# A spectral block with a Mish MLP on one core: column matrices by POOL's converting DMA, another order at the start

## The chip, the cores and the metric

The kernel runs on one core of one Trainium2 chip. The core has five engines that run side by side and wait for each other through semaphores: TensorE (PE in the profile; PEld is its loading of weights), VectorE (DVE), ScalarE (ACT), GpSimd (POOL) and SyncE (SP, which here only issues DMAs). Sixteen DMA engines move data between the chip's memory (HBM) and the core's. Each engine works through its own queue of instructions in order; an instruction that waits holds up all that stand behind it on that engine.

The metric is the device time of one execution in microseconds (us); lower is better. Three runs of the kernel before took 402.98, 403.83 and 403.90, median 403.83.

## The reference

The input x is 2048 rows of 512 numbers. Six rows of 512 numbers, `sa, ca, ga, sb, cb, gb`, are computed from a conditioning vector c.

```python
mod = (silu(c) @ w_mod).reshape(c.shape[0], 6, 1, -1)
h = layernorm(x) * (1 + ca) + sa
x = x + ga * irfft2(rfft2(h) * (w_r + 1j * w_i))      # over rows and columns
h = layernorm(x) * (1 + cb) + sb
x = x + gb * (mish(h @ w1 + b1) @ w2)                 # 512 -> 1376 -> 512
```

All is float32. The change lies in the forward transform `rfft2` (and, with one line, in the first product of `h @ w1`).

## The kernel before

**Stages.** The span has four: the forward transform of the rows and the first part of that of the columns (tiles n = 0 to 15, up to about 56 us), the rest of the column transform with the multiplication by the filter (to about 110), the inverse transform (to about 160), and the MLP in eight blocks (to the end). Each stage is written out by hand in the order in which its instructions stand in the queues (`tc.manual_schedule()`); nothing reorders them, and the framework adds the semaphore waits.

**The first stage.** Row 16 p + n of x stands on partition p of tile n, so a tile is 128 rows of 512 numbers. For every tile:

- `load_all` has SP issue three DMAs: `xring` (the tile of x, transposed on the host, eight buffers), `x` (the tile itself) and `mraw` (the tile's column matrix, 128 x 256: real and imaginary part; 128 KB).
- `norm_sums` takes mean and variance on DVE (L112, L113). `norm_guess` (ACT, L117 and L118) makes a first value of one over the deviation, `norm_refine` (DVE, three short instructions at L125) improves it, for two tiles at a time.
- `p1_row` is the row transform on PE (L192, four fp32 products; the matrix `krs` already holds the factor 1 + ca). `p1_mean` (DVE, L207) takes the mean's part away, with the row `kb` that `row_sums` and ACT's copy L203 made once.
- `p1_cast` and `p1_low` scale the result and split it in a high part `gh` and a low part `gl`, both float32r, the format in which PE takes 32-bit numbers in fewer passes: even tiles with ACT (L220) and DVE (L227), odd tiles with ACT (L216, L217) and POOL (L218).
- `p1_split` splits the column matrix in the same way: ACT casts `mraw` to the high part (L184), POOL subtracts for the low part (L185) and turns the sign of the imaginary parts (L186). The ring `mring` has eight buffers.
- `p1_col` is the column product on PE, nine matmuls: (high matrix, `gh`), (low matrix, `gh`), (high matrix, `gl`), each as L234, L235 and L236. `p1_save` (ACT, L240) takes the result out of PSUM.

In the loop, iteration n holds `p1_save(n-1)`, `p1_row(n+2)`, `p1_mean` and `p1_cast` of tile n + 1, `p1_low(n)`, `p1_col(n)`, `p1_split(n+3)` and `norm_sums(n+3)`.

**Before the loop.** c and the scale's weights `wmc` are loaded by ACT and SP, c is passed through silu (the last step is L298 on DVE, which makes `sc`), PE runs eleven products of ones (`warm`, L273), then sixteen products that give the scale as columns (`scale_sums`, L245, 128 equal columns of which one is used), and DVE makes `krs` from them (`scale_rows`, four at L250).

**The shift sums.** `mod_step` (DVE, L97 and L99) adds up the shift row sa from four pieces of `wms`: the pieces at iterations 12, 13, and the last two at 14. `shift_columns` after the loop needs the sum (PE, L104).

**DMA queues.** The framework has eight semaphores for the DMAs issued by SP and ACT, so a DMA waits until the one eight before it has landed. SP also issues, in the first stage, `wms` and the second stage's weights (`load_rest`: `kf`, `wz`, `wqa` and others). POOL issues no DMA in this kernel.

**The first product of the MLP.** `up(g)` multiplies by the high part of w1 (L729, 512 columns: high and low half of h) and by its low part (L731, the 256 columns of h's high half). `up(0)` and `up(1)` stand in the last tiles of the inverse transform, where `p3_row` (PE, L647) is followed by an addition to x on DVE (L650).

Of the kernel before, what the change touches and what calls it, by code (L numbers as in the profile page):

```python
# [7 lines left out]
F32 = mybir.dt.float32  # L8
F32R = mybir.dt.float32r
# [21 lines left out]
def tile_spectral_block(ctx: ExitStack, tc: tile.TileContext, x_d, w1_d, b1_d, w2_d,  # L31
# [24 lines left out]
    def plain(t):  # L56
        return t.bitcast(F32)
# [15 lines left out]
    eps = base.tile([P, 1], F32, name="eps")  # L73

    saz = base.tile([P, NQ], F32, name="saz")
    mraw = big.tile([P, N2, 256], F32, name="mraw", tag="da")
    mring = big.tile([P, 8, 2, 384], F32R, name="mring", tag="db")
    wmc = big.tile([P, 4, 512], F32, name="wmc", tag="cr")
    wms = big.tile([P, 4, 512], F32, name="wms", tag="ci")

# [29 lines left out]
    def norm_sums(n):  # L110
        t = small.tile([P, 6], F32, name="st")
        nc.vector.bn_stats(t, x[:, n, :])  # L112
        nc.vector.bn_aggr(mv[:, n, :], t)  # L113
# [31 lines left out]
        return h  # L145

    st = {}
    mkd = km_d.bitcast(F32R)

    def mt(n):  # L150
        return mring[:, n % 8]

    def load_m(n):
        nc.sync.dma_start(mraw[:, n, :], km_d[:, n, :])

    def load_x(n):
        nc.sync.dma_start(x[:, n:n + 1, :], xv[:, n:n + 1, :])

    def load_xt(n):
        t = xring[:, n % 8]  # L160
        nc.sync.dma_start(t, xt_d[n])
        st["xt", n] = t

    def load_all(n):
        load_xt(n)
        load_x(n)
        load_m(n)

    def load_rest():
        nc.sync.dma_start(ident, kp_d)  # L170
# [8 lines left out]
                nc.sync.dma_start(b1n[:, 0:NF - 1], b1_d[0:(NF - 1) * P].rearrange("(f p) -> p f", p=P))  # L179
                nc.sync.dma_start(b1n[0:F - (NF - 1) * P, NF - 1:NF], b1_d[(NF - 1) * P:F].unsqueeze(1))  # L180

    def p1_split(n):
        m = mt(n)
        nc.scalar.copy(m[:, 0, 0:256], mraw[:, n, :])  # L184
        nc.gpsimd.tensor_tensor(m[:, 1, 0:256], mraw[:, n, :], plain(m[:, 0, 0:256]), op=ALU.subtract)  # L185
        nc.gpsimd.tensor_scalar(m[:, :, 256:384], plain(m[:, :, 128:256]), -1.0, 0.0,  # L186
                                op0=ALU.mult, op1=ALU.add)

    def row_products(pg, data):
# [39 lines left out]
    def p1_col(n):  # L229
        m = mt(n)  # L230
        gh, gl = st.pop(("g", n))
        pa = bank("C")
        for i, (a, g) in enumerate(((0, gh), (1, gh), (0, gl))):
            nc.tensor.matmul(pa, m[:, a, 0:128], g, start=(i == 0), stop=False)  # L234
            nc.tensor.matmul(pa[:, 0:256], m[:, a, 256:384], g[:, 256:512], start=False, stop=False)  # L235
            nc.tensor.matmul(pa[:, 256:512], m[:, a, 128:256], g[:, 0:256], start=False, stop=(i == 2))  # L236
        st["pa", n] = pa

    def p1_save(n):
# [2 lines left out]
    def scale_sums(ks, ps):  # L242
        for k in ks:
            for j in range(4):
                nc.tensor.matmul(ps[j][:, 0:P], wmc[:, k, j * P:(j + 1) * P], sc[:, k:k + 1].to_broadcast([P, P]),  # L245
                                 start=(k == 0), stop=(k == 3))

    def scale_rows(ps):
        for j in range(4):
            nc.vector.scalar_tensor_tensor(krs[:, j, :], kr[:, j, :], ps[j][:, 0:1], kr[:, j, :],  # L250
                                           op0=ALU.mult, op1=ALU.add)
# [23 lines left out]
    with tc.manual_schedule():  # L275
        def load_scale(eng, k):
            eng.dma_start(wmc[:, k, :], wm_d[:, 1, k, :])

        nc.scalar.dma_start(sc, c_d.rearrange("b (p k) -> p (b k)", k=4))
        load_scale(nc.scalar, 1)  # L280
        load_scale(nc.scalar, 3)
        nc.scalar.preload_act_table_set("natural_log_exp_and_others")
        load_xt(0)
        load_scale(nc.sync, 0)
        load_scale(nc.sync, 2)
        nc.sync.dma_start(kr, kr_d)
        load_x(0)
        load_m(0)
        for n in range(1, 8):
            load_all(n)  # L290
        nc.vector.memset(ones, 1.0)
        nc.vector.memset(eps, EPS)
        nc.vector.memset(b1n[:, NF - 1:NF], 0.0)
        sg = small.tile([P, 4], F32, name="sg")
        nc.scalar.activation(sg, sc, AF.Exp, scale=-1.0)
        nc.vector.tensor_scalar(sg, sg, 1.0, None, op0=ALU.add)
        nc.vector.reciprocal(sg, sg)
        nc.vector.tensor_tensor(sc, sc, sg, op=ALU.mult)  # L298
        warm(11)
        cps = [bank(t) for t in "DDCC"]  # L300
        for k in range(4):
            scale_sums((k,), cps)
        norm_sums(0)
        norm_guess(0, 1)
        scale_rows(cps)
        norm_refine(0, 1, -1)
        p1_split(0)
        p1_row(0)
        load_all(8)
        row_sums()  # L310
        p1_row(1)
        load_all(9)
        norm_sums(1)
        norm_guess(1, 2)
        p1_mean(0)
        p1_cast(0)
        norm_refine(1, 2, -1)
        p1_split(1)
        p1_mean(1)
        p1_cast(1)  # L320
        p1_low(0)
        p1_split(2)
        norm_sums(2)
        for n in range(N2):
            if n >= 1:
                p1_save(n - 1)
            if n + 2 < N2:
                p1_row(n + 2)
                if n + 10 < N2:
                    load_all(n + 10)  # L330
                if n == 4:
                    nc.sync.dma_start(wms, wm_d[:, 0, :, :])
                if n == 6:
                    load_rest()
            if 1 <= n and n + 1 < N2:
                p1_mean(n + 1)
                if n % 2:
                    norm_refine(n + 1, n + 3, -1)
                p1_cast(n + 1)
            if n:  # L340
                p1_low(n)
            p1_col(n)
            if n + 3 < N2:
                p1_split(n + 3)
                norm_sums(n + 3)
                if n % 2 == 0:
                    norm_guess(n + 2, n + 4)
            for k in {12: (0,), 13: (1,), 14: (2, 3)}.get(n, ()):
                mod_step(macc, wms[:, k, :], k, nc.vector)
        p1_save(N2 - 1)  # L350
        shift_columns()

# [368 lines left out]
    def up(g):  # L721
        b, t = item(g)
        h = h2[b]
        ups[g] = []
        for e, f, rows in tiles(t):
            ps = bank("CD"[e] if g < 2 else "AD"[e])[:rows]
            fs = slice(f * P, f * P + rows)
            for k in range(4):
                nc.tensor.matmul(ps, w1h[:, k, fs], h[:, k], start=(k == 0), stop=False)  # L729
            for k in range(4):  # L730
                nc.tensor.matmul(ps[:, 0:256], w1l[:, k, fs], h[:, k, 0], start=False, stop=(k == 3))  # L731
            ups[g].append((e, f, ps))

    def front(g):
# [208 lines left out]
def _constants():  # L943
# [11 lines left out]
    kr = pair(unit(512, (4 * a[:, None, None] + d2[None, :, None]) * q), 2)  # L955
    kr[:, :, 1, 0] = alt[:, None]
    z = unit(2048, (16 * a[:, None, None] + k2[None, :, None]) * a)
    km = np.stack([z.real, z.imag], 2)
    z = np.conj(z).transpose(2, 1, 0)
    kc = np.stack([z.real, -z.imag], 1)  # L960
    z = 2 * np.conj(unit(512, (4 * a[None, None, :] + d2[None, :, None]) * q[:, None, None]))
# [57 lines left out]
    def bwd(n, fn):  # L1019
# [5 lines left out]
    out = dict(kr=kr.reshape(128, 4, 128), km=km.reshape(128, 16, 256), kc=kc,  # L1025
               ki=ki.reshape(128, 4, 128), kf=kf, kv=kv, kw=kw, kp=np.eye(128))
    return {k: np.ascontiguousarray(v, dtype=np.float32) for k, v in out.items()}

# [48 lines left out]
```

## Time and profile before

| | |
|---|---|
| median of three runs | 403.83 us (402.98 to 403.90) |
| profiled execution, its own time | 403.98 us |
| span of that execution | 402.0 us, granted TensorE clock 1.00 |
| busy: PE, DVE, ACT, POOL | 390.5, 305.0, 249.9, 99.2 us |
| DMA | 36.45 MB, mean 91 GB/s |
| DVE busy in 20 to 30, 30 to 40, 40 to 50 us | 9.64, 9.72, 9.79 of 10 us |
| PE busy in the same | 9.34, 9.34, 9.36 |
| POOL busy in the same | 8.27, 7.46, 7.40 |

The page of the profile shows one execution: the busy time of each engine, the span in 40 slices (a digit is the busy share in tenths), the DMA queues, the chain of waits that ended last, and the costliest groups of instructions. The timeline gives each instruction with its start and length in us; a bracket names the idle time of the engine before it and what ended it. Matmuls are pipelined and their ends are modelled, so the distance of two starts says more of PE than its busy time. A row of the windows view gives a stretch, its length, the busy time of PE, PEld, DVE, ACT and POOL with counts in parentheses, the granted clock, the busy share of the DMA engines and GB/s.

### The profile page before, as it was taken

The page shows a single profiled execution, that of the slowest core. Times are in us where ns is not written, and L with a number is a line of the kernel's source. Part 1 is how long each engine was busy: PE and PEld are TensorE (multiplying, and loading weights), DVE is VectorE, ACT ScalarE, POOL GpSimd, SP SyncE. Part 2 cuts the span into 40 slices and gives each one's busy share as a digit, 9 for nine tenths or more (in the row PEclk, how much of TensorE's full clock was granted, in tenths as well). Part 3 has the DMA queues.
Part 4 walks back from the last instruction along what each step waited for, and adds up shares of the span by engine and source line. Part 5 has one row for each costly group of instructions (what it writes and reads, how often), then busy time and mean ns, then how long its engine had stood idle before and what let it go on. Part 6 is the DMA issues. An engine that isn't in the chain of part 4 may idle for free.

```text
span 402.0 us, 7454 instructions
## 1 busy us (share of the span) xinstructions
PE 390.5 (97%) x2782; PEld 360.5 (90%) x2782; DVE 305.0 (76%) x653; ACT 249.9 (62%) x547; POOL 99.2 (25%) x132
## 2 busy tenths in 40 slices
PE   8999979999999999999999999999999999999996
PEld 8888868999899999899899899899899899999984
DVE  2899958786339999887974974974974974987994
ACT  2577753667746954896494494494484484494751
POOL 0587725666316762230000000000000010017000
PEclk9999999999999999999999999999999999999999
DMA  8999790454304331100010010010010020023011
GB/s 286 382 334 389 207 314 7 127 215 176 94 14 122 90 124 48 62 18 2 9 45 2 4 50 0 2 53 2 0 55 2 0 72 2 2 78 132 1 54 52
DMA packets 20580, 36.45 MB, mean 91 GB/s; under 512 B 3680, under 2 KB 6528, under 8 KB 20160
## 3 DMA queue, kind: packets, MB, share of 16 engines
q1 hardware_dynamic: 20112, 35.45, 25.9%
q8 instruction: 22, 0.36, 0.4%
q10 hardware_dynamic: 432, 0.53, 0.4%
q14 instruction: 14, 0.11, 0.1%
HBM read 31.78 MB, written 4.19 MB: 89 GB/s over the span
## 4 chain that ended last, share of the span: by engine, by line
PE 74%; DVE 19%; ACT 3%; issue 2%; POOL 1%; POOLq 0%; ACTq 0%
PE bank L782 23%; PE bank L729 19%; PE bank L731 10%; DVE st L112 4%; PE bank L456 3%; DVE ve L125 3%; PE bank L502 3%; PE bank L774 3%; DVE x L650 2%; PE bank L794 2%; PE bank L489 2%; PE bank L616 2%; PE bank L435 1%; DVE buf L227 1%; DVE buf L207 1%
## 5 line engine op out<-in xcount | busy, mean ns | idle before, releaser
L739 ACT ACTIVATE buf<-bank,b1n 128x256 f32<-128x256 f32 (+1 forms) x88 | 40.9, 472 | 66.9 <-PE bank L731 66.7
L740 DVE TENSOR_TENSOR buf<-buf,bank 128x256 f32<-128x256 f32 (+1 forms) x88 | 35.4, 417 | 38.9 <-ACT buf L739 38.9
L689 DVE TENSOR_TENSOR al<-buf,ah 128x512 fp32r<-128x512 f32 (+2 forms) x85 | 53.4, 651 | 1.8 <-ACT ah L688 1.8
L706 POOL TENSOR_TENSOR buf<-buf,modr 128x512 f32<-128x512 f32 (+1 forms) x3 | 3.9, 1292 | 183.5 <-DMA buf<-in_B_w_dram 183.5
L729 PE MATMUL bank<-h2e,w1h 128*128 128x512 f32 (+1 forms) x176 | 48.4, 397 | 0.0
L729 PE MATMUL bank<-h2o,w1h 128*128 128x512 f32 (+1 forms) x176 | 48.3, 396 | 0.0
L688 ACT CAST ah<-buf 128x512 fp32r<-128x512 f32 (+2 forms) x85 | 43.0, 549 | 0.7 <-DVE buf L756 0.6
L756 DVE TENSOR_TENSOR buf<-buf 128x128 f32<-128x128 f32 x148 | 39.3, 307 | 3.5 <-ACT buf L746 2.2
L746 ACT ACTIVATE buf<-buf 128x512 f32<-128x512 f32 (+1 forms) x48 | 28.7, 598 | 14.9 <-DVE buf L740 14.8
L782 PE MATMUL bank<-w2a,ah 128*128 128x256 f32 x161 | 34.9, 286 | 0.0
L729 PEld LDWEIGHTS bank<-h2o,w1h 128*128 128x128 f32 (+1 forms) x176 | 30.2, 187 | 4.5
L729 PEld LDWEIGHTS bank<-h2e,w1h 128*128 128x128 f32 (+1 forms) x176 | 30.1, 187 | 4.5
L782 PE MATMUL bank<-w2b,ah 128*128 128x256 f32 x147 | 31.8, 283 | 0.0
L731 PEld LDWEIGHTS bank<-h2e,w1l 128*128 128x128 f32 (+1 forms) x176 | 26.7, 185 | 4.2
L731 PEld LDWEIGHTS bank<-h2o,w1l 128*128 128x128 f32 (+1 forms) x176 | 26.7, 185 | 4.2
L731 PE MATMUL bank<-h2e,w1l 128*128 128x256 f32 (+1 forms) x176 | 27.8, 280 | 0.0
L731 PE MATMUL bank<-h2o,w1l 128*128 128x256 f32 (+1 forms) x176 | 27.8, 280 | 0.0
L782 PEld LDWEIGHTS bank<-w2a,ah 128*128 128x128 f32 x161 | 26.7, 191 | 0.0
L234 PE MATMUL bank<-buf,mring 128*128 128x512 f32 x48 | 21.4, 446 | 4.2 <-DVE buf L227 1.9
L637 PE MATMUL bank<-kc,d 128*128 128x128 f32 x128 | 24.9, 276 | 0.5 <-ACT d L360 0.5
L638 PE MATMUL bank<-kc,d 128*128 128x128 f32 x128 | 24.8, 275 | 0.0
L112 DVE BATCH_NORM_STATS2 st<-x 128x6 f32<-128x512 f32 x32 | 22.0, 688 | 3.5 <-DMA x<-in_A_x_dram 3.1
(221 smaller groups left out, 1026.1 us busy)
## 6 DMA issues: line engine op xcount, KB each, us to landing
buf<-in_B_w_dram SPq DMA_DIRECT2D x20, 256.0 KB, 2.7
xring<-in_x_t_dram SPq DMA_DIRECT2D x16, 256.0 KB, 4.6
x<-in_A_x_dram SPq DMA_DIRECT2D x16, 256.0 KB, 4.8
wm<-in_w_mod_dram SPq DMA_DIRECT2D x16, 256.0 KB, 4.3
out_dram<-x SPq DMA_DIRECT2D x7, 512.0 KB, 2.6
mraw<-in_km_dram SPq DMA_DIRECT2D x16, 128.0 KB, 4.5
wqa<-in_w_q_dram SPq DMA_DIRECT2D x8, 256.0 KB, 4.6
wqb<-in_w_q_dram SPq DMA_DIRECT2D x8, 256.0 KB, 3.9
```

The costliest lines, as they stand in the source:

```text
L112: nc.vector.bn_stats(t, x[:, n, :])
L637: nc.tensor.matmul(o, dj[:, 0:128], kc[0][:, n, :], start=True, stop=False)
L638: nc.tensor.matmul(o, dj[:, 64:192], kc[1][:, n, :], start=False, stop=True)
L688: nc.scalar.copy(h, r)
L689: nc.vector.tensor_tensor(l, r, plain(h), op=ALU.subtract)
L729: nc.tensor.matmul(ps, w1h[:, k, fs], h[:, k], start=(k == 0), stop=False)
L731: nc.tensor.matmul(ps[:, 0:256], w1l[:, k, fs], h[:, k, 0], start=False, stop=(k == 3))
L739: nc.scalar.activation(o, ps[:, 256:], AF.Identity, bias=b1n[:rows, f:f + 1])
L740: nc.vector.tensor_tensor(o, o, ps[:, 0:256], op=ALU.add)
L746: nc.scalar.activation(o, o, AF.Mish)
L756: nc.vector.tensor_tensor(o, p, q, op=op)
L782: nc.tensor.matmul(o, a[p][:, e], w2[t][q][:, r], start=(own and half == 0 and t == 1 and i == 0), stop=(end and i == 2 and (n, half) != ( ...
```

## The change

- The column matrix of a tile is split in its high and low part on the host, so the DRAM tensor `km` holds 512 numbers per row and tile in place of 256 (256 KB a tile), and it is loaded straight into the float32r tiles `mh` by DMAs that POOL issues, since source (float32) and target (float32r) have different types. Nine DMAs: tiles 0 and 1 alone, then two tiles each; no ring is needed, as `mh` holds all sixteen. `p1_split` becomes `p1_turn`, which only turns the signs (one POOL instruction); ACT's cast and POOL's subtraction are gone, and so are SP's sixteen loads of `mraw`.
- `scale_sums` uses 64 equal columns in place of 128, and the last step of silu runs on POOL.
- At the start SP loads the scale's weights and `kr` before the first tile. On DVE `scale_rows` comes before the first tile's statistics; on PE `row_sums` before `p1_row(0)`; `norm_refine`, mean and cast of tile 0 come before the statistics of tile 1.
- In POOL's queue the order is: `sc`, load of m0, `p1_turn(0)`, loads of m1 and of m2 with m3, `p1_turn(1)`, load of m4 with m5, the low part of tile 1's data, `p1_turn(2)`, `p1_turn(3)`, load of m6 with m7, `p1_turn(4)`, the low part of tile 3's data, and so on with a load at every even iteration.
- `mod_step` runs one piece at each of the iterations 11 to 14.
- In `up(0)` alone, the products with w1's low part are made in two halves of 128 columns: eight matmuls in place of four.

```diff
-    mraw = big.tile([P, N2, 256], F32, name="mraw", tag="da")
-    mring = big.tile([P, 8, 2, 384], F32R, name="mring", tag="db")
+    mh = [big.tile([P, 8, 768], F32R, name=f"mh{i}", tag=t) for i, t in enumerate(("da", "db"))]
...
     def mt(n):
-        return mring[:, n % 8]
+        return mh[n // 8][:, n % 8]
...
-    def load_m(n):
-        nc.sync.dma_start(mraw[:, n, :], km_d[:, n, :])
+    def load_m(lo, hi):
+        nc.gpsimd.dma_start(mh[lo // 8][:, lo % 8:lo % 8 + hi - lo, 0:512], km_d[:, lo:hi, :])
...
     def load_all(n):
         load_xt(n)
         load_x(n)
-        load_m(n)
...
-    def p1_split(n):
+    def p1_turn(n):
         m = mt(n)
-        nc.scalar.copy(m[:, 0, 0:256], mraw[:, n, :])
-        nc.gpsimd.tensor_tensor(m[:, 1, 0:256], mraw[:, n, :], plain(m[:, 0, 0:256]), op=ALU.subtract)
-        nc.gpsimd.tensor_scalar(m[:, :, 256:384], plain(m[:, :, 128:256]), -1.0, 0.0,
+        nc.gpsimd.tensor_scalar(m[:, 512:768].rearrange("p (a k) -> p a k", a=2),
+                                plain(m[:, 0:512]).rearrange("p (a c k) -> p a c k", a=2, c=2)[:, :, 1], -1.0, 0.0,
                                 op0=ALU.mult, op1=ALU.add)
...
-                nc.tensor.matmul(ps[j][:, 0:P], wmc[:, k, j * P:(j + 1) * P], sc[:, k:k + 1].to_broadcast([P, P]),
+                nc.tensor.matmul(ps[j][:, 0:64], wmc[:, k, j * P:(j + 1) * P], sc[:, k:k + 1].to_broadcast([P, 64]),
...
-        load_xt(0)
         load_scale(nc.sync, 0)
         load_scale(nc.sync, 2)
         nc.sync.dma_start(kr, kr_d)
-        load_x(0)
-        load_m(0)
+        load_all(0)
...
-        nc.vector.tensor_tensor(sc, sc, sg, op=ALU.mult)
+        nc.gpsimd.tensor_tensor(sc, sc, sg, op=ALU.mult)
+        load_m(0, 1)
         warm(11)
         cps = [bank(t) for t in "DDCC"]
         for k in range(4):
             scale_sums((k,), cps)
+        p1_turn(0)
+        load_m(1, 2)
+        load_m(2, 4)
+        scale_rows(cps)
         norm_sums(0)
         norm_guess(0, 1)
-        scale_rows(cps)
-        norm_refine(0, 1, -1)
-        p1_split(0)
+        row_sums()
         p1_row(0)
         load_all(8)
-        row_sums()
         p1_row(1)
         load_all(9)
+        norm_refine(0, 1, -1)
+        p1_mean(0)
+        p1_cast(0)
         norm_sums(1)
         norm_guess(1, 2)
-        p1_mean(0)
-        p1_cast(0)
+        p1_turn(1)
+        load_m(4, 6)
+        p1_mean(1)
         norm_refine(1, 2, -1)
-        p1_split(1)
-        p1_mean(1)
         p1_cast(1)
         p1_low(0)
-        p1_split(2)
+        p1_turn(2)
...
             if n + 3 < N2:
-                p1_split(n + 3)
+                p1_turn(n + 3)
                 norm_sums(n + 3)
                 if n % 2 == 0:
                     norm_guess(n + 2, n + 4)
-            for k in {12: (0,), 13: (1,), 14: (2, 3)}.get(n, ()):
-                mod_step(macc, wms[:, k, :], k, nc.vector)
+            if n % 2 == 0 and n + 6 < N2:
+                load_m(n + 6, n + 8)
+            if 11 <= n < 15:
+                mod_step(macc, wms[:, n - 11, :], n - 11, nc.vector)
...
             for k in range(4):
-                nc.tensor.matmul(ps[:, 0:256], w1l[:, k, fs], h[:, k, 0], start=False, stop=(k == 3))
+                for c in range(0, 256, 256 if g else P):
+                    v = slice(c, c + (256 if g else P))
+                    nc.tensor.matmul(ps[:, v], w1l[:, k, fs], h[:, k, 0, v], start=False, stop=(k == 3 and v.stop == 256))
...
-    km = np.stack([z.real, z.imag], 2)
+    km = np.stack([z.real, z.imag], 2).reshape(128, 16, 256)
+    bits = km.astype(np.float32).view(np.uint32)
+    high = ((bits + 0x7FF + ((bits >> 12) & 1)) & 0xFFFFF000).astype(np.uint32).view(np.float32)
+    km = np.concatenate([high, km - high], 2)
```

More of the change, by code (lines that the diff above doesn't have):

```diff
@@ L147, in tile_spectral_block @@
     st = {}
-    mkd = km_d.bitcast(F32R)
     def mt(n):
-        return mring[:, n % 8]
-    def load_m(n):
-        nc.sync.dma_start(mraw[:, n, :], km_d[:, n, :])
+        return mh[n // 8][:, n % 8]
+    def load_m(lo, hi):
+        nc.gpsimd.dma_start(mh[lo // 8][:, lo % 8:lo % 8 + hi - lo, 0:512], km_d[:, lo:hi, :])
     def load_x(n):
@@ L233, in p1_col @@
         for i, (a, g) in enumerate(((0, gh), (1, gh), (0, gl))):
-            nc.tensor.matmul(pa, m[:, a, 0:128], g, start=(i == 0), stop=False)
-            nc.tensor.matmul(pa[:, 0:256], m[:, a, 256:384], g[:, 256:512], start=False, stop=False)
-            nc.tensor.matmul(pa[:, 256:512], m[:, a, 128:256], g[:, 0:256], start=False, stop=(i == 2))
+            re, im, neg = (m[:, c:c + P] for c in (256 * a, 256 * a + 128, 512 + 128 * a))
+            nc.tensor.matmul(pa, re, g, start=(i == 0), stop=False)
+            nc.tensor.matmul(pa[:, 0:256], neg, g[:, 256:512], start=False, stop=False)
+            nc.tensor.matmul(pa[:, 256:512], im, g[:, 0:256], start=False, stop=(i == 2))
         st["pa", n] = pa
@@ L1024, in _constants @@
     kw = np.concatenate([m[128:] for m in zero], 1)
-    out = dict(kr=kr.reshape(128, 4, 128), km=km.reshape(128, 16, 256), kc=kc,
+    out = dict(kr=kr.reshape(128, 4, 128), km=km, kc=kc,
                ki=ki.reshape(128, 4, 128), kf=kf, kv=kv, kw=kw, kp=np.eye(128))
```

## The prediction

> **What bounds the kernel now.** The page's slices come first: how busy VectorE (DVE) and the DMA engines are along the span, in tenths.
>
> ```profile
> DVE  2899958786339999887974974974974974987994
> DMA  8999790454304331100010010010010020023011
> ```
>
> A slice is 10 us. The change works in the first six, the forward transform; in slices 2 to 5 both rows stand near nine, and TensorE (PE) is at 9.3 of 10 there (the window of 30 to 40 us, below), so no share says which one binds. The chain of waits does (start, length, what), cut to one period of two tiles:
>
> ```profile
> 34.76 0.61 DVE st L112
> ...
> 38.04 0.30 ACT rstd L117
> ...
> 38.61 0.46 DVE ve L125
> 39.09 0.68 DVE ve L125
> 39.79 0.16 DVE rstd L125
> 39.95 0.61 DVE st L112
> ```
>
> 39.95 - 34.76 = 5.19 us for two tiles, nearly all on DVE, with the short `ve` as long as a 512-column instruction. The timeline of that stretch shows why (start, length, engine, line):
>
> ```profile
> 15.03 0.75 DVE L227 SCALAR_TENSOR_TENSOR buf<-buf,rstd 128x512 fp32r<-128x512 f32 x1
> ...
> 33.44 0.47 PE L234 MATMUL bank<-buf,mring 128*128 128x512 f32 x1
> 33.82 0.74 POOL L185 TENSOR_TENSOR mring<-mraw,mring 128x256 fp32r<-128x256 f32 x1
> 33.91 0.66 DVE L125 SCALAR_TENSOR_TENSOR ve<-ve,rstd 128x2 f32<-128x2 f32 x1
> 34.46 0.40 PE L234 MATMUL bank<-buf,mring 128*128 128x512 f32 x1
> 35.74 0.47 PE L234 MATMUL bank<-buf,mring 128*128 128x512 f32 x1
> 35.90 0.74 POOL L185 TENSOR_TENSOR mring<-mraw,mring 128x256 fp32r<-128x256 f32 x1 [0.85 <-ACT mring L184]
> 36.13 1.05 DVE L227 SCALAR_TENSOR_TENSOR buf<-buf,rstd 128x512 fp32r<-128x512 f32 x1
> 37.24 0.50 PE L234 MATMUL bank<-buf,mring 128*128 128x512 f32 x1 [0.33 <-DVE buf L227]
> 38.63 0.48 PE L234 MATMUL bank<-buf,mring 128*128 128x512 f32 x1
> ```
>
> The `ve` that takes 0.66 ends at 34.57, as POOL's subtraction L185 ends (34.56); the last L125 of the period, at 39.79 in the chain, takes 0.16. L227 takes 1.05 when it meets the next L185, and 0.75 at 15.03, where no POOL instruction is under way as it starts. So L185 holds DVE 0.50 + 0.30 = 0.80 us per pair, and PE waits for L227. PE's own need: col(7) to col(8) takes 35.74 - 33.44 = 2.30 us without a wait, col(8) to col(9) 38.63 - 35.74 = 2.89 with one. In the first the product with `gl` comes 34.46 - 33.44 = 1.02 after the first product, in the second 37.24 - 35.74 = 1.50, so 0.48 is stall: PE needs 2.30 + 2.41 = 4.7 us per pair.
>
> **The change part by part.**
>
> *Splitting.* L184 (ACT's cast) and L185 (POOL) go, 16 of each; the turned copy L186 stays. DVE per pair: 5.19 - 0.80 = 4.39, below PE's 4.7, so PE is late next and a pair costs 4.7. DVE still meets POOL's L218, which I leave in; for what it and ACT's steps still cost PE I take 4.8, and keep 4.7 and 5.0 for the range. The starts of columns and the waits of PE over the stage:
>
> ```profile
> 17.21 0.47 PE L234 MATMUL bank<-buf,mring 128*128 128x512 f32 x1
> 18.22 0.46 PE L234 MATMUL bank<-buf,mring 128*128 128x512 f32 x1
> 23.59 0.44 PE L234 MATMUL bank<-buf,mring 128*128 128x512 f32 x1
> 49.00 0.47 PE L234 MATMUL bank<-buf,mring 128*128 128x512 f32 x1
> 55.62 0.50 PE L234 MATMUL bank<-buf,mring 128*128 128x512 f32 x1 [0.58 <-POOL buf L218]
> PE bank L234 <- ACT buf L220: 1.6, 2, 1.2
> ```
>
> col(1) starts at 17.21, col(13) at 49.00: 31.8 us for six pairs. Six times 4.8 is 28.8: 3.0 gained (3.6 at 4.7, 1.8 at 5.0).
>
> *Shift sums.* Before, the first `mod_step` and then the last two on one tile stand in DVE's queue before work that PE awaits: ACT's 1.2 us wait above is col(14), and the last L218 is late. Now one follows each of tiles 11 to 14. The same four instructions, of which DVE's new slack of some 0.3 per pair carries a part, and the last is still queued behind tile 14's L227, near the last L218. From 49.00 to the last `gl` product at 55.62 are 6.6 us; PE alone needs two tiles of 2.3 and the 1.02 to that product, 5.6 us. I take 0.6 of that 1.0; ends 0 and 1.0.
>
> *The start.*
>
> ```profile
> 4.56 0.16 DVE L298 TENSOR_TENSOR sc<-sc,sg 128x4 f32<-128x4 f32 x1
> 5.91 4.04 PE L245 MATMUL bank<-sc,wmc 128*128 128x128 f32 x32
> 9.32 1.84 DVE L250 SCALAR_TENSOR_TENSOR modr<-kr,bank 128x128 f32<-128x128 f32 x4 [0.56 <-PE bank L245]
> 12.63 0.59 ACT L203 COPY modr<-bank 128x512 f32<-128x512 f32 x1 [3.01 <-PE bank L192]
> 14.80 0.50 PE L234 MATMUL bank<-buf,mring 128*128 128x512 f32 x1 [0.43 <-ACT buf L220]
> 56.36 0.79 PE bank L104 x8
> ```
>
> `scale_sums` at 64 columns: 4.04 / 32 = 0.126 each at 128 columns, and 0.79 / 8 = 0.099 at one column (L104), so 26 of them end 0 to 0.7 earlier; I take 0.10, and L250 starts near 8.6. Before, the copy L203 starts 12.63 - 11.16 = 1.5 after L250, behind two sets of products. The new order has x's statistics (0.61, some 0.2 for the aggregate) and ACT's two guesses (0.30 each) there, 1.4, so col(0) comes near 14.1, 0.7 earlier, its mean done near 13.3. But before `gl(0)` now stand the statistics and mean of tile 1 and its refining: 13.3 + 0.8 + 0.7 + 0.5 = 15.3 against 15.03. col(0) can't end without it, so the start is worth -0.3; ends -0.8 and +0.5.
>
> *sc on POOL.* 0.16 us on DVE, ended at 4.72, becomes between that and L185's 0.74 on POOL, 5.3 at the latest. PE's warm-up covers it to 5.9; past that it is paid one for one.
>
> *The loads.* SP loses 16 issues and reaches x sooner. POOL gains nine DMAs, of which the trace shows none. The nearest rows are POOL's own work, and the landing of the same matrices (`mraw`, 16 issues by SP), SP's issue of `wms`, and the windows:
>
> ```profile
> 9.69 0.83 POOL L185 TENSOR_TENSOR mring<-mraw,mring 128x256 fp32r<-128x256 f32 x1 [9.24 <-ACT mring L184]
> 37.77 1.28 POOL L218 TENSOR_TENSOR buf<-buf 128x512 fp32r<-128x512 f32 x1 [0.31 <-ACT buf L217]
> ...
> DMA to landing us min/median/max: 4.3/4.5/6.8
> L332 SPq DMA_DIRECT2D wms<-in_w_mod_dram x1: 328/328/328, 30.1 to 30.1; - x1
> 30.00:40.00 10.00, 9.34 (x68) 8.41 (x66) 9.72 (x21) 7.78 (x19) 7.46 (x10) 1.00 1.04 389
> 47.50:50.00 2.50, 2.39 (x17) 2.26 (x18) 2.47 (x5) 1.84 (x5) 2.18 (x3) 1.00 0.04 14
> ```
>
> Issuing holds POOL between 0.33 (SP's 328 ns) and 1.28 (L218): I take 1.0 as for POOL's ordinary work, half a pair's slack, since POOL had 7.5 us of work in ten and loses 1.5 per pair. L, from issue to landing, I take as 4.5. POOL's queue is serial: m0 is issued at 4.8, turn(0) waits for it, then m1 goes, turn(1), then m4, and turn(4) stands before `gl(3)`. So m1 lands at 5.4 + 2L = 14.4, turn(1), an issue and L218 give `gl(1)` at 8.2 + 2L = 17.2 (its product now: 18.22), and `gl(3)` is done at 7.6 + 3L = 21.1 (now: 23.59). Hidden, with 1.0 and 2.5 us in hand.
>
> 2.1 MB more at 389 GB/s is 5.4 us of DMA, in a stretch whose window shows the engines full (share 1.04). What is issued before the gap at 47.5 to 50 (0.04), the next stage's weights with it, is in by 47.5 now and by 53 then; first use is at 62.1 (the next fence), some 59 after the gain. The shift matrix `wms`, issued at 30.1 and with that landing's longest 6.8 in by 37, has 12 x 256 KB of m ahead of it instead of 15 x 128: 1.2 MB, 3 us, so 40. Its new use, behind col(11), was at 49.00 - 5.19 = 43.8 and moves to some 43: hidden, with no more than that in hand.
>
> *up(0).* Four 256-column products become eight of 128.
>
> ```profile
> L472 DVE TENSOR_TENSOR buf<-bank,wqa x12: 548/681/692, 62.1 to 73.2; 128x512 f32<-128x512 f32 x10, 128x384 f32<-128x384 f32 x2
> 155.48 0.63 PE L731 MATMUL bank<-h2e,w1l 128*96 128x256 f32 x4
> 155.95 1.05 PE L647 MATMUL bank<-kiv,buf 128*128 128x128 f32 x8
> 157.47 0.65 DVE L650 TENSOR_TENSOR x<-x,bank 128x512 f32<-128x512 f32 x1
> ```
>
> The four take 0.47, and fp32 products of 128 columns two records of 1.05 / 8: 0.26 each. Eight thus cost 0.47 to 2.1; L650 leaves 157.47 - 157.0 = 0.47 free. Cost 0 to 1.2; I take 0, by the row of the same type.
>
> **Sum.** 3.0 + 0.6 - 0.3 = 3.3 us. The profiled execution took 403.98 (span 402.0): 400.7. The median of the runs is 403.83, 0.15 lower: 400.5. After the stage, PE and DVE chains wait for no DMA that the change touches, so the gain is carried to the end.
>
> **Rivals.**
> 1. *POOL's queue delivers late (slower).* If L is near the rows' 6.8 rather than 4.5, `gl(3)` comes at 28.0, 4.4 us after today's 23.59. What is won after it, 5 pairs x 0.4 + 0.6 = 2.6, leaves +1.8: 405.6. It decides from 7.6 + 3L = 26.2, L = 6.2. For it: the row's maximum, software issue, nine transfers against full DMA engines. Against it: SP's 4.5 is that of a queue always filled with transfers; POOL's holds two or three. The Trainium skill (DMA: Bandwidth & Descriptors, Anatomy of one DMA — SWDGE (gpsimd) path) fits 2.0 us plus the bytes over 436 GB/s to a DMA of POOL's; by that page an estimate of 2.6 us for 256 KB, with which this rival falls and the sum stays.
> 2. *Issuing on POOL holds DVE as L185 did (slower).* One issue of up to 1.28 per pair makes 4.39 + 1.28 = 5.67, 0.48 over today's: 6 x 0.48 + 0.3 - 0.6 = +2.6, 406.4. From 0.8 on it costs. For: every POOL instruction with SBUF operands does so here. Against: an issue reads no tile. The Trainium skill (SBUF — State Buffer, Who interferes with whom) has a two-input DVE instruction held only by POOL work that reads SBUF; by that rule the sum stays 400.5, and no run yet shows it.
> 3. *POOL's first instruction starts late (less gain).* In the trace POOL's first instruction after the constants is at 9.69, behind ACT's cast, so it isn't shown ready at 4.7. Were it ready at 7, `scale_sums` would start at 7.1 instead of 5.9: 1.2 lost, 401.7. The Trainium skill (GPSIMD Engine Reference, 2.1 Instruction dispatch) gives the first call to a freshly loaded kernel about 6 us; by it the time is this rival's.
> 4. *Nothing moves.* PE's pair stays at 5.2 because x, with 768 KB per tile instead of 640 on full engines, comes no faster: at 389 GB/s 2.0 us per tile against 2.4 needed speaks against it. 403.8.
>
> **How the numbers follow.** The forecast has 0.48, rival 3 0.09, rival 1 0.21, rival 2 0.13, rival 4 0.07, other losses 0.02. Under 0.3% (1.2 us) a measurement of this kernel can hardly tell a difference. Faster 0.57, same 0.07, slower 0.36. The forecast's own range: gain 1.8 + 0 - 0.8 = 1.0 to 3.6 + 1.0 + 0.5 = 5.1, so 398.7 to 402.8. The slower rivals hold 0.34, so the range reaches to them: 398.7 to 406.5.
>
> **What would show it.** Right: no DVE L125 over 0.5 us beside POOL; L227 at 0.75; pairs of columns 4.7 to 4.8 apart; the last `gl` product near 52.3; L250's first near 8.6. Wrong: PE waiting for POOL's turn or `gl` in tiles 1 to 4; DVE instructions that end with a POOL issue; a POOL idle until 6 or 7; DVE held by the shift matrix near 43.

## The result, and the profile after

Five runs of the changed kernel took 405.90 to 407.31 us, median 406.03; five of the kernel before 402.33 to 403.90, median 402.98. The ratio is 1.008 (95% interval 1.0055 to 1.0105): the change costs about 3 us, where a gain of 3.3 was forecast. The profiled execution took 406.28 us with a span of 404.5.

Lines have moved: L227 is now L222, L125 L124, L207 L202, L218 L213, L234 L230, L186 (the turned copy) L180, L250 L246, L245 L241, L117 L116; POOL's DMAs are L151.

The chain of waits of the first 21 us (start, length, what) is no longer one of computing:

```profile
5.10 6.48 DMA mh<-in_km_dram
...
11.67 0.36 POOL mh L180
12.02 5.97 DMA mh<-in_km_dram
...
18.07 0.40 POOL mh L180
18.47 0.72 POOL mh L151
19.21 1.29 POOL buf L213
20.54 0.71 PE bank L230
```

POOL issues the load of m0, waits for it, turns it, and only then issues the load of m1, waits for that, turns it, issues the next load, and only then makes `gl(1)` (L213), for which TensorE waits. The timeline of PE shows what that does to the columns (each row here is the first or the `gl` product of a column; bracket: idle before, and what ended it):

```profile
14.11 0.50 PE L230 MATMUL bank<-buf,mh 128*128 128x512 f32 x1 [0.23 <-ACT buf L215]
18.12 0.47 PE L230 MATMUL bank<-buf,mh 128*128 128x512 f32 x1 [0.35 <-ACT rstd L116]
...
27.77 0.50 PE L230 MATMUL bank<-buf,mh 128*128 128x512 f32 x1 [0.78 <-POOL buf L213]
...
43.08 0.50 PE L230 MATMUL bank<-buf,mh 128*128 128x512 f32 x1 [0.97 <-POOL buf L213]
...
52.03 0.48 PE L230 MATMUL bank<-buf,mh 128*128 128x512 f32 x1
...
57.99 0.50 PE L230 MATMUL bank<-buf,mh 128*128 128x512 f32 x1 [0.17 <-POOL buf L213]
```

Column 0 starts at 14.11, 0.7 earlier than before. The product with `gl(3)` is at 27.77, 4.2 later than before (23.59). Column 13 starts at 52.03 instead of 49.00, the last `gl` product is at 57.99 instead of 55.62, and the span is 2.5 longer. So TensorE was 4.2 late after the first four tiles, and 1.8 of it was won back by the end of the stage. The loads were late once more behind that: the product with `gl(9)`, at 43.08, waited 0.97, since POOL had stood 3.48 us for a load of m in front of a turned copy at 41.39.

The page's list of DMAs gives the median from issue to landing:

```profile
x<-in_A_x_dram SPq DMA_DIRECT2D x16, 256.0 KB, 6.6
...
mh<-in_km_dram POOLq DMA_DIRECT2D x7, 512.0 KB, 7.6
...
mh<-in_km_dram POOLq DMA_DIRECT2D x2, 256.0 KB, 6.2
```

The two transfers of 256 KB that open the chain took 6.2 at the median, the seven of 512 KB 7.6. The prediction's sum took 4.5 for both. Even x, issued by SP as before, lands later; the same row of the kernel before is

```profile
x<-in_A_x_dram SPq DMA_DIRECT2D x16, 256.0 KB, 4.8
```

After the start, DVE did not become as free as forecast either (timeline of DVE and POOL in the changed kernel):

```profile
30.66 1.27 POOL L213 TENSOR_TENSOR buf<-buf 128x512 fp32r<-128x512 f32 x1
30.94 1.02 DVE L124 SCALAR_TENSOR_TENSOR ve<-mv,rstd 128x2 f32<-128x2 f32 x1
...
36.05 0.77 DVE L124 SCALAR_TENSOR_TENSOR ve<-mv,rstd 128x2 f32<-128x2 f32 x1
```

The short `ve` ends as POOL's L213 ends (31.96 and 31.93), and from one to the next are 36.05 - 30.94 = 5.11 us per pair of tiles, hardly less than the 5.19 before. The forecast was 4.39 for DVE. The columns did come closer together there, 36.07 - 31.46 = 4.61 per pair from column 5 to column 7, at a time when TensorE was late and DVE's work for it had been done.

Two questions follow: is it the order of the loads that costs, or their bytes; and what holds DVE now that L185 is gone?

### The profile page after: what moved, and what is told of

Its sections match the earlier page's. It is cut to its first block, busy times and chain, and to the rows that moved or that the text cites. A ratio compares the mean times of both kernels' runs of the same rounds, so it can differ in the third digit from the quotient of the medians.

```text
span 404.5 us, 7424 instructions
## 1 busy us (share of the span) xinstructions
PE 391.8 (97%) x2786; PEld 362.2 (90%) x2786; DVE 302.0 (75%) x652; ACT 245.1 (61%) x531; POOL 91.9 (23%) x126
## 4 chain that ended last, share of the span: by engine, by line
PE 81%; DVE 8%; DMA 4%; ACT 3%; POOL 3%; issue 2%; POOLq 0%; ACTq 0%
PE bank L784 23%; PE bank L729 20%; PE bank L733 10%; DMA mh<-in_km_dram 3%; PE bank L456 3%; PE bank L502 3%; PE bank L647 3%; PE bank L637 2%; PE bank L776 2%; PE bank L638 2%; PE bank L796 2%; PE bank L616 2%; POOL buf L213 2%; PE bank L489 2%; PE bank L435 1%
## 5 line engine op out<-in xcount | busy, mean ns | idle before, releaser
L784 PE MATMUL bank<-w2b,ah 128*128 128x256 f32 x147 | 31.8, 283 | 0.0
L733 PE MATMUL bank<-h2e,w1l 128*128 128x256 f32 (+2 forms) x180 | 28.0, 278 | 0.0
L230 PE MATMUL bank<-buf,mh 128*128 128x512 f32 x48 | 21.8, 455 | 5.5 <-POOL buf L213 3.0
L784 PEld LDWEIGHTS bank<-w2b,ah 128*128 128x128 f32 x147 | 24.6, 191 | 0.0
```

The lines of the kernel that those rows point to most:

```text
L230: nc.tensor.matmul(pa, re, g, start=(i == 0), stop=False)
L733: nc.tensor.matmul(ps[:, v], w1l[:, k, fs], h[:, k, 0, v], start=False, stop=(k == 3 and v.stop == 256))
L784: nc.tensor.matmul(o, a[p][:, e], w2[t][q][:, r], start=(own and half == 0 and t == 1 and i == 0), stop=(end and i == 2 and (n, half) != ( ...
```

## The experiments

**Loads ahead.** The same transfers, issued earlier:

```diff
         load_m(0, 1)
+        load_m(1, 2)
+        load_m(2, 4)
+        load_m(4, 6)
...
         p1_turn(0)
-        load_m(1, 2)
-        load_m(2, 4)
...
         p1_turn(1)
-        load_m(4, 6)
+        load_m(6, 8)
...
-            if n % 2 == 0 and n + 6 < N2:
-                load_m(n + 6, n + 8)
+            if n % 2 == 0 and n + 8 < N2:
+                load_m(n + 8, n + 10)
```

> The changed kernel with its loads of m issued ahead: the first four (6 tiles) one behind the other in front of the first turned copy, and each later pair two tiles earlier. Same transfers, same bytes, same work. Theory A (POOL's queue is serial, and m1 is only issued when the turned copy of m0 is done): the four go at 5.1, 5.9, 6.7 and 7.4 us, land with the measured 6.2 to 7.6 us by 11.6, 12.5, 14.3 and 15.0; the product with gl(1) comes near 18 instead of 20.5, that with gl(3) near 23 or before instead of 27.8, and the time is 400.5 to 402. Theory B (the bytes are late, whatever their order, because the 16 DMA engines are full): the landing time rises with the number of transfers under way, to 10 us and more, gl(3) still comes after 26 and the time stays within 1 us of 406.0.

It took 402.97 us (402.46 to 403.64), ratio to before 0.9987 (0.9976 to 0.9998). That is 0.9% under the changed kernel, so the serial queue is shown as the cause of its loss: `gl(1)` is used at 18.65 instead of 20.54, `gl(3)` at 24.08 instead of 27.77 (theory A had said 23 or before), and POOL's waits for m between 5 and 62 us (in all, how often, the longest) shrink from the first of these rows, the changed kernel's, to the second:

```profile
POOL mh L180 <- DMA mh<-in_km_dram: 20.5, 7, 5.8
```

```profile
POOL mh L180 <- DMA mh<-in_km_dram: 4.7, 2, 3.7
```

The landing did rise, from 6.2 to 6.6 us (256 KB) and from 7.6 to 8.9 (512 KB): theory B is right in sign, but `gl(3)` came before its 26 and the time is 3 us under 406.0.

But 400.5 to 402 was expected. The timeline shows why it was missed:

```profile
17.64 0.47 PE L230 MATMUL bank<-buf,mh 128*128 128x512 f32 x1
...
32.49 1.28 POOL L213 TENSOR_TENSOR buf<-buf 128x512 fp32r<-128x512 f32 x1 [2.29 <-DVE mv L112]
33.03 0.77 DVE L124 SCALAR_TENSOR_TENSOR ve<-mv,rstd 128x2 f32<-128x2 f32 x1
33.76 0.40 POOL L180 TENSOR_SCALAR mh<-mh 128x256 fp32r<-128x256 f32 x1
33.83 0.33 DVE L124 SCALAR_TENSOR_TENSOR ve<-ve,rstd 128x2 f32<-128x2 f32 x1
34.11 0.78 POOL L151 DMA_DIRECT2D mh<-in_km_dram  x1
34.20 0.42 DVE L124 SCALAR_TENSOR_TENSOR rstd<-ve,rstd 128x2 f32<-128x2 f32 x1
...
48.63 0.47 PE L230 MATMUL bank<-buf,mh 128*128 128x512 f32 x1
...
54.59 0.50 PE L230 MATMUL bank<-buf,mh 128*128 128x512 f32 x1 [0.17 <-POOL buf L213]
```

From column 1 to column 13 are 48.63 - 17.64 = 31.0 us, 5.17 per pair (31.8 before, 28.8 forecast). The first L124 runs until L213 ends (33.77), the second until the turned copy ends (34.16), the third takes 0.42 beside the issue, behind which the next turned copy follows at 34.92. Undisturbed, each takes 0.16. So 0.77 + 0.33 + 0.42 - 0.48 = 1.04 us of hold is left in this pair. Before it was 1.10: the 0.80 of L185, and 0.30 by which L218 already held the first of the three (0.46 at 38.61 in the prediction's chain). L185's 0.80 went (L222 is down to 0.75 in the mean), and what POOL does next took nearly all of it over.

**All loads at the start.** The same edit, with all nine `load_m` in front of the first turned copy and none later.

> The changed kernel with all nine loads of m issued one behind the other in front of the first turned copy; none is issued later. Theory A: no turned copy waits after the first few, the time is that of the run with six tiles ahead, or up to 1 us better if waits for m were left in that one. Theory B: x shares the DMA engines with 4 MB of m at the start (4 MB at 389 GB/s is 10.3 us), the statistics of tiles 1 to 4 wait for x by several us, and the time is above the changed kernel's 406.0.

404.23 us (403.26 to 404.72), ratio 1.0023 (1.001 to 1.0035): 1.3 us above the run before, though below 406.0. From 12 us on only one turned copy waits for m (1.7 us), but now x is late. From its waits between 12 and 58 us, and its list of DMAs:

```profile
DVE st L111 <- DMA x<-in_A_x_dram: 3.6, 7, 0.7
```

```profile
mh<-in_km_dram POOLq DMA_DIRECT2D x7, 512.0 KB, 15.8
```

Seven of DVE's statistics wait for x, 3.6 us in all, against one of 0.4 in the run before. The large transfers of m are under way for 15.8 us, and x's last load is issued at 36.0 instead of 33.5. That m takes x's share of the DMA engines fits this; it was not measured by itself. Theory A missed (the time is not better), and of theory B the late x came without its 406.0: the order of the loads decides, and too early costs as well as too late.

**A transfer without traffic.** One more DMA of 256 KB on POOL's queue, in two of every block's six steps of the last stage.

```diff
         up(s)
+        if b < NB - 1 and i in (2, 5):
+            nc.gpsimd.dma_start(quiet, km_d[:, 0:1, :])
```

> The changed kernel with one more transfer of 256 KB of m by POOL's queue, into a tile that nothing reads, in two of each block's six steps in the last stage (from 170 us on), where the DMA engines are busy 0 to 0.1 of the time. It prices the landing without traffic: if the 6.2 us of the start is waiting behind full DMA engines, it lands in 2 to 3.5 us here (SP's transfers of 256 KB take 2.7 there); if POOL's software path is slow by itself, in 5 us or more. It shows as well whether an issue on POOL holds DVE (rival 2): DVE is busy 0.8 of that time, and an instruction of two inputs beside an issue would take 0.7 us longer than its group's median.

From the trace of the tile `quiet`, and the timeline:

```profile
DMA to landing us min/median/max: 2.8/3.0/4.6
```

```profile
200.08 1.23 DVE L829 TENSOR_TENSOR modr<-modr 128x1024 f32<-128x1024 f32 x1
200.18 0.53 POOL L843 DMA_DIRECT2D quiet<-in_km_dram  x1 [2.77 <-DMA quiet<-in_km_dram]
```

Quiet, POOL's DMA lands in 3.0 us; SP's of the same size took 2.7. So POOL's path is not slow by itself: of the 6.2 us of the chain, 3.2 come with the traffic of the start, where the DMA engines are full (share 1.15 in the window of 18 to 20 us at the end of this document). And an issue that lies wholly beside a DVE instruction with both inputs in SBUF leaves it at 1.23, its group's median; L690 at 187.10, with two such inputs as well, takes 0.69 beside the issue at 187.06, where its group's mean is 0.71. In these rows issuing alone does not hold DVE. The execution took 407.7, with its additions.

**Shift sums alone.** On the kernel before:

```diff
-            for k in {12: (0,), 13: (1,), 14: (2, 3)}.get(n, ()):
-                mod_step(macc, wms[:, k, :], k, nc.vector)
+            if 11 <= n < 15:
+                mod_step(macc, wms[:, n - 11, :], n - 11, nc.vector)
```

> The kernel before with only the shift sums spread over tiles 11 to 14. By the prediction's step the stretch from the start of column 13 to the last product with gl is 6.0 instead of 6.6 us, and the span 0.6 shorter (401.4). Rival: DVE, held by L185, has no slack for them there, the products with gl of tiles 12 to 14 come later by what the sums take (up to 0.7 each), and the span is that of before or longer.

402.67 us in its one execution, which lies within the times of the kernel before (402.41 to 404.51). Column 13 starts at 47.96, the last `gl` product is at 54.40: 6.44 us instead of 6.62, so 0.2 of the 0.6 expected. With the loads ahead the same stretch is 54.59 - 48.63 = 5.96, and 57.99 - 52.03 = 5.96 in the changed kernel. That fits the rival's reason, that DVE has little room for the sums while L185 holds it; no run takes the hold alone away. (The span of this execution, 400.7, is not its doing: column 1 already starts 1.1 earlier, since PE's warm-up took 4.07 us in it and 5.06 in the profiled execution of before. The same warm-up takes 4.21 in the run with all loads at the start and 5.07 in the one with the loads ahead.)

**Turned copies on ScalarE.** With the loads ahead,

```diff
-        nc.gpsimd.tensor_scalar(m[:, 512:768]...
...
+        to = m[:, 512:768].rearrange("p (a k) -> p a k", a=2)
+        im = plain(m[:, 0:512]).rearrange("p (a c k) -> p a c k", a=2, c=2)[:, :, 1]
+        if n < 3:
+            nc.gpsimd.tensor_scalar(to, im, -1.0, 0.0, op0=ALU.mult, op1=ALU.add)
+        else:
+            nc.scalar.mul(to, im, -1.0)
```

> The run with the loads ahead, and the turned copies of tiles 3 to 15 made by ScalarE instead of POOL. Nothing on the critical path waits for a turned copy there, so a gain can only come from what POOL's copy does to others. Theory C (DVE still bounds the stage, at 5.1 us per pair, since its three short L124 are held by whatever POOL runs: 0.60 by L213, 0.17 and 0.26 by the turned copies): without the copies DVE needs 5.12 - 0.43 = 4.7 per pair, as much as TensorE, the six pairs from column 1 to column 13 take 28.2 to 29 us instead of 31.0, and the time falls by 1.5 to 2.5 us to 400.5 to 401.5. Rival D (TensorE or ScalarE sets the pace, DVE's long L124 only fill time it has): six pairs stay at 31 us or more, since ScalarE gains 0.8 us of work per pair, and the time is 403 or above.

400.86 us (400.23 to 401.16), ratio 0.9948 (0.9928 to 0.9967): within the 400.5 to 401.5 of theory C. In the timeline (L216 is here POOL's subtraction for `gl`, L233 the product):

```profile
17.49 0.48 PE L233 MATMUL bank<-buf,mh 128*128 128x512 f32 x1
...
31.35 1.27 POOL L216 TENSOR_TENSOR buf<-buf 128x512 fp32r<-128x512 f32 x1 [2.72 <-DVE mv L112]
32.03 0.61 DVE L124 SCALAR_TENSOR_TENSOR ve<-mv,rstd 128x2 f32<-128x2 f32 x1
32.58 0.74 POOL L151 DMA_DIRECT2D mh<-in_km_dram  x1
32.68 0.16 DVE L124 SCALAR_TENSOR_TENSOR ve<-ve,rstd 128x2 f32<-128x2 f32 x1
32.88 0.16 DVE L124 SCALAR_TENSOR_TENSOR rstd<-ve,rstd 128x2 f32<-128x2 f32 x1
...
46.38 0.47 PE L233 MATMUL bank<-buf,mh 128*128 128x512 f32 x1
...
52.18 0.50 PE L233 MATMUL bank<-buf,mh 128*128 128x512 f32 x1 [0.16 <-POOL buf L216]
```

Six pairs take 46.38 - 17.49 = 28.89 us, 4.82 each. TensorE waits for no turned copy in either run, and ScalarE has more to do. What changed for DVE is that the second and third L124 are back at 0.16, beside the issue too; the first is still held by L216 (0.61, where it was 0.77). TensorE's loads of weights wait for the `gl` of DVE (us in all, how often, the longest; 12 to 58 us), first with the loads ahead, then here:

```profile
PEld bank L230 <- DVE buf L222: 3.7, 8, 1.0
```

```profile
PEld bank L233 <- DVE buf L225: 2.0, 4, 1.0
```

For POOL's `gl` they wait 0.6 in both, so it isn't POOL's own queue that became shorter for them. That the copies held DVE, and DVE the stage, is shown.

**The low parts on DVE.** With the loads ahead, gl of every tile made by DVE as for the even ones; POOL's subtraction and ScalarE's second copy go.

```diff
-        if n % 2:
-            g = buf("t")
-            nc.scalar.activation(g, c, AF.Copy, scale=one)
-            nc.scalar.copy(gh, g)
-            nc.gpsimd.tensor_tensor(gl, g, plain(gh), op=ALU.subtract)
-        else:
-            nc.scalar.activation(gh, c, AF.Copy, scale=one)
+        nc.scalar.activation(gh, c, AF.Copy, scale=one)
...
-        if n % 2 == 0:
-            gh, gl = st["g", n]
-            nc.vector.scalar_tensor_tensor(gl, c, rstd[:, n:n + 1], plain(gh), op0=ALU.mult, op1=ALU.subtract)
+        gh, gl = st["g", n]
+        nc.vector.scalar_tensor_tensor(gl, c, rstd[:, n:n + 1], plain(gh), op0=ALU.mult, op1=ALU.subtract)
```

> The run with the loads ahead, and gl of the odd tiles made by DVE as of the even ones (POOL's subtraction L213 and ScalarE's extra copy go; the turned copies stay on POOL). Theory C: DVE gains an instruction of 0.66 and loses L213's hold of 0.60, which leaves 5.12 + 0.06 less what of the turned copies' 0.43 no longer meets a short instruction: 4.8 to 5.2 per pair, time 401 to 403. Rival D: DVE has 0.66 more per pair, the six pairs take 34 us, time 406.

402.03 us (400.81 to 402.44), ratio 0.9977 (0.9964 to 0.9989): theory C's 401 to 403, and far from rival D's 406. The pairs fit less well: six take 48.45 - 16.49 = 31.96 us, 5.33 each, above theory C's 4.8 to 5.2. The first of them takes 6.95, since TensorE waits 2.07 for `gl(1)`, which DVE now makes behind its other work, with 0.7 us of waiting for x in it; the five after it take 5.00 each. DVE gets one more large instruction per pair (0.75) and the kernel becomes no slower: the hold that goes was worth as much.

**Both.** From tile 3 on POOL computes nothing in this stage.

> Both: from tile 3 on POOL only issues transfers, no compute instruction of it runs from then to the end of the stage. Theory C: DVE has its unheld sum, 4.04 + 0.66 + 0.1 for the gaps = 4.8 per pair, with L124 at 0.16 each and L202 and L222 at 0.66 to 0.75; six pairs 28.8, time 400.5 to 401.5, the same as with the turned copies alone moved. Rival E (the issues of POOL's transfers hold DVE too): L124 of 0.5 us or more remain beside the issues.

402.24 us (401.91 to 403.16), ratio 0.9986 (0.9976 to 0.9996): 0.7 above the upper end of theory C. From 15.5 us to the end of the stage every L124 takes 0.16, the one at 18.34 beside an issue too, so rival E finds nothing. But six pairs take 48.64 - 17.55 = 31.09 us and not 28.8. The first takes 5.74: TensorE waits 0.89 for `gl(1)`, which DVE makes here. More of what was missed stands in POOL's timeline and in the waits between 12 and 58 us:

```profile
15.54 2.91 POOL L151 DMA_DIRECT2D mh<-in_km_dram  x4
```

```profile
DVE st L111 <- DMA x<-in_A_x_dram: 0.9, 2, 0.6
```

With no work of its own between them, POOL issues its last four transfers from 15.5 us on, and x is late as in the run with all at the start: its last load is issued at 35.8, and the two waits stand before DVE's work for `gl(5)` and `gl(7)`, in pairs that take 5.56 and 5.31. The pair from column 9 to column 11, where nothing is late, takes 43.66 - 38.92 = 4.74, theory C's 4.8. No run takes the two causes apart.

**ScalarE, with the loads of the changed kernel.** The edit of the turned copies alone.

> The changed kernel with its own order of loads, and the turned copies of tiles 3 to 15 on ScalarE. If the two losses (late loads, some 3 us; DVE held, some 2 us) are separate, the late start stays (gl(3) after 26, column 4 near 29) and the pairs behind it come at 4.7 to 4.8: column 13 near 50.6 instead of 52.0, time 404 to 405. Rival: the turned copy waits for m in ScalarE's queue as it did in POOL's, with the casts behind it; the waits of POOL for m come back on ScalarE and the time is 406 or above.

409.62 us (408.80 to 410.18), ratio 1.0159 (1.0136 to 1.0182). The rival is right: `gl(3)` comes at 29.55, and column 13 at 56.17 where 50.6 was expected. Two of the waits from 5 to 75 us:

```profile
DVE ve L124 <- ACT rstd L117: 10.7, 6, 4.4
ACT mh L185 <- DMA mh<-in_km_dram: 10.5, 5, 5.0
```

A turned copy (here L185) that waits for m in ScalarE's queue holds the guesses and casts behind it. The two remedies aren't independent: the second is a gain only once the first is in.

**ScalarE, on the kernel before.** Only L186 of tiles 3 to 15 moved.

> The kernel before with only the turned copies (L186) of tiles 3 to 15 on ScalarE; split and loads as they were. It asks whether what the turned copies cost is new with the change. By theory C the instructions that hold DVE in the kernel before are L185 (0.80 per pair) and L218 (0.30), not L186: pairs stay at 5.1 to 5.3, time within 1 us of before. Rival: any POOL work taken away frees DVE here as well: 4.8 per pair and 400.5 to 401.5, so that the change of the split was not needed for it.

418.81 us (418.18 to 419.82), ratio 1.0393 (1.0366 to 1.0421): both expectations missed. The row

```profile
ACT mring L190 <- POOL mring L185: 18.6, 13, 2.9
```

tells why: the copy needs the low part from L185, and ScalarE, waiting for POOL 13 times, holds the casts that feed POOL and PE. Whether L186 held DVE before the change therefore stays open.

**The first tile's work in the order of before**, on the version with loads ahead and turned copies on ScalarE.

> The fastest run so far (loads ahead, turned copies of tiles 3 to 15 on ScalarE) with the first tile's work in the order of before. By the prediction's step the new order makes column 0 earlier by 0.7 and column 1 later by 0.3: here column 0 near 14.8, column 1 near 17.2 instead of 17.5, time 400.5 to 400.8. Rival: the new order is worth something after column 1 (x's statistics come sooner); the time is 401.2 or above.

400.85 us (400.04 to 402.88), ratio 0.9946 (0.9927 to 0.9966), against 400.86. Column 0 starts at 14.61 and column 1 at 17.02, 0.55 later and 0.47 earlier than there, with the signs that the step has; in time it is nothing, and the rival's 401.2 isn't reached. Its profiled execution, 402.88, is the slowest of its runs: x is late in it, by 4.7 us at the first tile's statistics and by 1.9 at 20.55, and the others can't be shown to have that.

## Why the prediction was wrong, by its own steps

**The loads: the step that failed first.** "L, from issue to landing, I take as 4.5" was a row of another queue in a stage with fewer bytes. Measured: 6.2 for the first two, 7.6 for the others at the median, and rival 1 had said that it decides from 6.2. The formulas around it held: `gl(1)` done at 8.2 + 2 x 6.2 = 20.6 (measured 20.48), `gl(3)` at 7.6 + 6.2 + 6.2 + 7.6 = 27.6 (27.72). So the loads weren't "hidden, with 1.0 and 2.5 us in hand" but 2.3 and 4.2 late, which is rival 1: it had `gl(3)` at 28.0. That its 405.6 lies so near 406.03 is in part luck: it is 1.8 above 403.83, while the span became 2.5 longer and the medians of the comparison lie 3.05 apart. The price of moving m to POOL lay in the same sum: with 2.1 MB more in full engines the landings were longer, x's 6.6 instead of 4.8, and a chain counts each of them. Nor did SP reach x sooner: its last load is issued at 32.1, before at 31.6. Against the rival the prediction cited the Trainium skill (DMA: Bandwidth & Descriptors, Anatomy of one DMA — SWDGE (gpsimd) path): 2.6 us for 256 KB by that fit. The quiet transfers, 3.0, come near it; those of the chain, behind traffic, don't.

**Splitting: the step that failed second.** "DVE per pair: 5.19 - 0.80 = 4.39, below PE's 4.7, so PE is late next" subtracts L185's hold and keeps the rest as it stood. L227 did fall to the 0.75 that was said (L222), but the short ones did not become free. The hold belongs to no one instruction: in these runs an L124 that comes while L213 or a turned copy is under way ends with it. POOL's remaining instructions moved up to that place, the hold went from 1.10 to 1.04 in the pair shown with the loads ahead instead of to 0.30, and the six pairs won 0.8 (31.8 to 31.0) instead of 3.0. With the turned copies out of POOL they won 2.9 (28.89). The Trainium skill (SBUF — State Buffer, Who interferes with whom) says that a DVE instruction with two inputs in SBUF contends with a POOL instruction that reads SBUF. The trace agrees: L124 has two such inputs and is held to the end of L213 or of a copy; L202, with one input in PSUM, takes 0.72 at 32.35 in the run with the loads ahead, beside the same L213 (0.719 in the mean). By that rule L213 and the turned copies were candidates from the start; the prediction used it for the issue alone, in rival 2.

**Rival 2** (the issue holds DVE) falls by the quiet run and by the L124 of 0.16 beside issues in the run with the turned copies on ScalarE; four slower ones stay open (last section). **Rival 3** falls: POOL's first instruction starts when its input is there. The 6 us of the Trainium skill (GPSIMD Engine Reference, 2.1 Instruction dispatch) aren't seen. The rows of the start, in the changed kernel:

```profile
4.58 0.20 POOL L292 TENSOR_TENSOR sc<-sc,sg 128x4 f32<-128x4 f32 x1 [4.13 <-DVE sg L291]
5.92 4.21 PE L241 MATMUL bank<-sc,wmc 128*128 128x64 f32 x32
9.50 1.16 DVE L246 SCALAR_TENSOR_TENSOR modr<-kr,bank 128x128 f32<-128x128 f32 x4 [5.05 <-PE bank L241]
```

**Rival 4** named late x as a way to nothing; in the changed kernel x wasn't what DVE waited for, but in the runs that issue m earliest it was.

**The start.** Right in sum, not in its parts. 64 columns cost 4.21 / 32 = 0.132 each, no less than the 0.126 of 128 (over the runs the 32 take 3.68 to 4.30 at 64 columns, 3.81 and 4.04 at 128), so L246 begins at 9.50 and not near 8.6; but its four follow each other in 1.16 instead of 1.84. Column 0 came at 14.11 (said: 14.1), `gl(0)` 0.32 later than before (said: 0.3).

**Shift sums.** 0.66 (6.62 to 5.96) against 0.6; but with L185 in place this part alone gave 0.2, so it seems to need the slack of DVE that the removal of L185 left. `wms` landed at 38.2 and was first used at 48.8: hidden.

**up(0).** The eight short products cost, in its timeline,

```profile
157.16 0.86 PE L729 MATMUL bank<-h2e,w1h 128*96 128x512 f32 x3
157.86 0.82 PE L733 MATMUL bank<-h2e,w1l 128*96 128x128 f32 x8
...
158.51 1.10 PE L647 MATMUL bank<-kiv,buf 128*128 128x128 f32 x8
```

158.51 - 157.16 = 1.35 us from the second of the four products with w1's high part (the row leaves out the first) to the next `p3_row`, 155.95 - 154.79 = 1.16 before: 0.2, where 0 was taken.

With both causes removed the prediction's sum nearly comes out in the profiled executions: 2.9 (pairs) + 0.8 (from column 13 to the last `gl` product, 5.80 instead of 6.62) - 0.3 (column 1 at 17.49 instead of 17.21) = 3.4, and that execution's span is 398.5, 3.5 under the 402.0 of before. The two executions flatter it, though: before took 403.98 in its one, at the upper end of its times, and this kernel 400.23, the lowest of its five. By the medians the gain is 2.1 (0.33% to 0.72%) of the 3.3 forecast; where the rest went isn't shown.

## What to carry to other kernels

When loads move to an engine that also computes, write its queue down as a chain (issue, landing, compute, next issue), and price each landing with the traffic the change itself adds; then issue a few transfers ahead of the first instruction that waits, but not so many that they crowd out what else must come. A hold between engines isn't removed with the instruction that showed it: ask which instruction of the same engine will stand there next. And an instruction that waits, moved to another engine, takes its wait along.

## What was not expected of the hardware

TensorE's granted clock fell to half for about 3.4 us after a stretch of short waits. Windows of the changed kernel (us, busy of PE, PEld, DVE, ACT, POOL, then the clock, DMA share, GB/s):

```profile
18.00:20.00 2.00, 1.37 (x6) 0.91 (x6) 1.93 (x4) 0.73 (x3) 1.90 (x3) 1.00 1.15 374
20.00:21.00 1.00, 0.46 (x1) 0.41 (x2) 1.00 (x2) 0.45 (x1) 0.49 (x1) 0.83 1.06 404
21.00:22.00 1.00, 1.00 (x6) 0.95 (x5) 0.96 (x4) 0.56 (x2) 0.44 (x2) 0.50 1.07 406
```

It stays at 0.50 to 24 us and is 0.96 in the mean of the next. From 12 us on no single wait of PE before it was longer than 1.05 us; the eight row products that follow took 1.91 instead of 1.05. The Trainium skill (TensorE: Matmul & The Clock Gate, Why this matters for your kernels) warns of gaps of TensorE above some 3 us. This trace has the fall without such a gap; what set it off isn't shown. It isn't the cause of the result: another execution of the changed kernel had a mean clock of 1.00, a span of 404.1 and 405.90 us.

One thing stays open. A third L124 at 18.71 in the changed kernel takes 1.81 us: it begins beside an issue and ends with the L213 behind it, while other L124 beside issues take 0.16. With the loads ahead, four third L124 stand beside an issue with a turned copy right behind it: three take 0.40 to 0.42 (at 19.10, 29.07 and 34.20), the one at 24.21 takes 0.16. So a POOL instruction behind the issue does not explain it alone, and no run tried it by itself.
